# Forward FFT convolution: turning h and the tables on the matrix engine, groups in a written-out software pipeline, MLP weights loaded and turned meanwhile

## The chip, the cores and the metric

One core of one Trainium2 chip runs the whole program as one launch. The metric is the device time in microseconds (us). Five engines work from queues of their own: PE (matrix multiply, with its weight loads shown as PEld), DVE (vector), ACT (scalar, activation functions), POOL (general purpose) and SP (here only a queue that issues transfers). POOL issues transfers too. An engine runs its queue in order and waits on semaphores.

## What is computed

Sequence S=2048, width D=512, MLP width F=1376, bf16. Four layers with the same two sublayers, and the gradients of all inputs (11 outputs):

```python
def A(q, k, v, shift_k, ssm_k, ssm_D):     # q = layernorm(x)
    kv = causal_conv4(k, shift_k) * v
    y  = irfft(rfft(pad(kv)) * rfft(pad(ssm_k)))[:S]   # long convolution, 2S points
    return q * (y + kv * ssm_D)
def B(x): return gelu(x @ w1 + b1) @ w2 + b2
x = q
x = x + A(layernorm(x)); x = x + B(layernorm(x))
x = x + A(layernorm(x)); x = x + B(layernorm(x))
out, vjp = jax.vjp(f, all inputs); return out, *vjp(grad_out)
```

Since k, v and the filter h (`ssm_k`, given as D x S) do not depend on x, y is computed once and kept in SBUF as `y_res`.

## The kernel before

**Convolution forward** (`phase_conv_forward`). The transform of 4096 points is done by products with tables. `Fold` splits a signal's eight blocks into sums and differences (`fold_x`, `fold_s`, `fold_d`, `fold_t`); its `streams(k1)` gives the four operands for one residue class. The 16 tiles of frequencies lie in five `GROUPS` of 2, 2, 4, 4, 4 tiles. `fwd_group` multiplies a group's streams by a table into PSUM (`sp_ps`) and ACT evicts it (spectrum `Hg` of h, `KVg` of kv). `product` multiplies the two on DVE (`pr_t`, `pr_u`) into `Yg`; `inv_group` multiplies `Yg` by the inverse table `tabI` (`iv_ps`), evicted by ACT into the slots of `W`; `inv_blocks` and two more operations combine W into y on DVE.

The tables are sines, made by `sin_of` in pieces of 1024 columns: a multiply-add on POOL, a mask on DVE, a sine on ACT, through two buffers `tab_u`. `tabN` serves h, `tabF` serves kv. h must be read with time on partitions, and also reversed: it is turned by four transposing transfers, stored (`hT_d`), read back in flipped order (`hB_d`) and loaded. `tabI` (from `tabF_d`), `tabG` (for the backward, from `tabN_d`) and the turned k (`kT_d`) are made by four transposing transfers each, issued by SP, in `y_res` as scratch for the last two. In program order: tables, k slices (`kt_ps`: turn k; `ks_ps`: the four-tap filter as products with `wdiag`), kv, then all five H groups, stored to `Hspec_d`, then the five kv groups, each one whole: load H, spectrum, product, inverse. The order on each engine is set by the tile framework's scheduler.

**MLP forward and backward** (`phase_mlp`). `load_weights` loads w1, w2 and turns them by 15 transposing transfers on SP (L718, L720: `w2T_sb` in 11, `w1T_sb` in 4), then centres the rows of w1T on DVE (L724 to L726). `interleave` runs four token slices through the layers: layer norm (L757), turn n by transposing transfers (`nT_sl`), z, gelu, o, with n, h and gelu' stored to DRAM (`n_d`, `h_d`, `gp_d`). Then the output gradient is loaded into `G`, and the backward runs in the same way (`gT_sl`, `gh_ps`, `gz_sl`, L869).

**Convolution backward** (`conv_backward`) runs the same transforms for the gradients, with the weight gradients (`weight_grads`) put between its steps by hand; PE is pinned to program order there by `Ordered`. The gradient of the four-tap filter is 16 multiply-accumulates of 128 x 2048 on DVE (L612).

Of the kernel before, what the change touches and what calls it, by code (L numbers as in the profile page):

```python
# [11 lines left out]
ACT = mybir.ActivationFunctionType  # L12
# [59 lines left out]
def ssm_kernel(ctx, tc: tile.TileContext, aps: dict):  # L72
# [13 lines left out]
    dram.tabN = drampool.tile([P, 2, 2, 2048], BF16, name="tabN_d")  # L86
# [3 lines left out]
    dram.tabG = drampool.tile([P, 2, 16, 256], BF16, name="tabG_d")  # L90
    dram.kT = drampool.tile([P, ND, S], BF16, name="kT_d")
    dram.hT = drampool.tile([S + 1, D], BF16, name="hT_d")
    dram.ks = drampool.tile([P, NT, D], BF16, name="ks_d")
    for nm in ("vB", "qB", "goB", "hB", "o0B", "o1B", "o3B"):
        setattr(dram, nm, drampool.tile([4, 256, D], BF16, name=f"{nm}_d"))
# [4 lines left out]
    dram.gp = {li: drampool.tile([P, NFC, S], BF16, name=f"gp{li}_d") for li in (1, 3)}  # L100
    phase_conv_forward(nc, tc, dims, consts, dram, res, aps)
# [67 lines left out]
def sin_of(nc, consts, pool, out, krow, pv, shift, np_=P):  # L169
    n = krow.shape[-1]  # L170
    for c0 in range(0, n, 1024):
        w = min(1024, n - c0)
        u = pool.tile([P, 1024], I32, name="tab_u", tag="tab_u", bufs=2)[0:np_, 0:w]
        nc.gpsimd.tensor_scalar(out=u, in0=krow[:, c0:c0 + w], scalar1=pv, scalar2=float(shift), op0=ALU.mult,
                                op1=ALU.add)
        nc.vector.tensor_single_scalar(out=u, in_=u, scalar=8191, op=ALU.bitwise_and)
        nc.scalar.activation(out=out[:, c0:c0 + w], in_=u, func=ACT.Sin, scale=SIN_SCALE, bias=consts.pibias[0:np_, :])

# [25 lines left out]
class Fold:  # L204
# [14 lines left out]
    def streams(self, k1):  # L219
# [9 lines left out]
        if k1 == 1:  # L229
            nc.vector.tensor_scalar(out=D[:, :, 1], in0=D[:, :, 1], scalar1=C8, scalar2=None, op0=ALU.mult)  # L230
# [4 lines left out]
        tt(out=T[:, 0], in0=e0, in1=D[:, 0, 1], op=op)  # L235
        tt(out=T[:, 3], in0=o0, in1=D[:, 1, 1], op=op)
# [9 lines left out]
def fwd_group(nc, psum, tab, st, g, out, extra=None):  # L246
    k1, base, n = GROUPS[g]
    for mt in range(n):
# [19 lines left out]
        nc.scalar.activation(out=out[:, :, mt, :], in_=ps, func=ACT.Identity)  # L268


def product(nc, pool, A, B, Rb, g, out, conj):
# [4 lines left out]
    for h in range(0, n, 2):  # L276
# [3 lines left out]
        u = pool.tile([P, 2, 2, 512], BF16, name="pr_u", tag="pr_u", bufs=2)  # L280
# [46 lines left out]
def inv_blocks(nc, W, PN, MW, last=False):  # L327

    tt = nc.vector.tensor_tensor
    tt(out=PN, in0=W[:, :, 4:6], in1=W[:, :, 6:8], op=ALU.add)  # L330
    tt(out=MW, in0=W[:, :, 4:6], in1=W[:, :, 6:8], op=ALU.subtract)
    G, B0, B1 = W[:, :, 4:6], W[:, :, 6:8], W[:, :, 2:4]
    tt(out=G[:, :, 0], in0=W[:, :, 0], in1=W[:, :, 1], op=ALU.add)
    tt(out=G[:, :, 1], in0=W[:, :, 0], in1=W[:, :, 1], op=ALU.subtract)
    tt(out=B0, in0=G, in1=W[:, :, 2:4], op=ALU.add)
    tt(out=B1, in0=G, in1=W[:, :, 2:4], op=ALU.subtract)
    tt(out=G[:, :, 0], in0=PN[:, :, 1], in1=MW[:, :, 0], op=ALU.add)
    tt(out=G[:, :, 1], in0=PN[:, :, 1], in1=MW[:, :, 0], op=ALU.subtract)
    nc.vector.tensor_scalar(out=G, in0=G, scalar1=C8, scalar2=None, op0=ALU.mult)
    tt(out=W[:, :, 0], in0=B0[:, :, 0], in1=PN[:, :, 0], op=ALU.add)  # L340
    tt(out=W[:, :, 1], in0=B0[:, :, 1], in1=G[:, :, 0], op=ALU.add)
    tt(out=W[:, :, 2], in0=B1[:, :, 0], in1=MW[:, :, 1], op=ALU.add)
# [6 lines left out]
def phase_conv_forward(ctx, nc, tc, dims, consts, dram, res, aps):  # L349
# [4 lines left out]
    tt = nc.vector.tensor_tensor  # L354
    psum = ctx.enter_context(tc.tile_pool(name="cf_ps", bufs=1, space=bass.MemoryType.PSUM))
    rstack = ExitStack()
    tabs = rstack.enter_context(tc.tile_pool(name="cf_tab", bufs=1, side="right"))
    tabF = tabs.tile([P, 2, 2, 2048], BF16, name="tabF")
    kv = tabs.tile([P, NT, D], BF16, name="kv")
    hrot = rstack.enter_context(tc.tile_pool(name="cf_rot", bufs=1, side="right"))  # L360
    fold_stack = ExitStack()
    foldp = fold_stack.enter_context(tc.tile_pool(name="cf_fold", bufs=1, side="right"))

    gen = ExitStack()
    gp = gen.enter_context(tc.tile_pool(name="cf_gen", bufs=1))
# [7 lines left out]
    pv5 = iota_f32(nc, gp, [5, 1], [[0, 1]], -512, 1024, "pv5")  # L373
    nc.vector.memset(pv5[0:1, :], 0.0)
# [3 lines left out]
    hT = gp.tile([P, NT, D], BF16, name="hT")  # L378
    hB = gp.tile([P, 4, 2, D], BF16, name="hB")
    hsp = gp.tile([5, D], BF16, name="hsp")  # L380
    zrow = gp.tile([1, D], BF16, name="zrow")
    nc.vector.memset(zrow, 0.0)

    ks_stack = ExitStack()
    kp = ks_stack.enter_context(tc.tile_pool(name="cf_k", bufs=1))
    flip_rows(nc, dram.vB, v_ap, 511)
    kns = []
    for i in range(2):
        kns.append(kp.tile([P, 4, D], BF16, name="kn", tag="kn", bufs=2))
        nc.sync.dma_start(out=kns[i], in_=k_ap[512 * i:512 * i + 512, :].rearrange("(t p) d -> p t d", p=P))  # L390
    wsh = kp.tile([P, ND, 4], BF16, name="wsh")
    nc.sync.dma_start(out=wsh, in_=aps["A_shift_k"].rearrange("(c p) j -> p c j", p=P))
    for cc in range(ND):
        nc.sync.dma_start_transpose(out=hT[:, :, cc * P:(cc + 1) * P], in_=h_ap[cc * P:(cc + 1) * P, :])
    nc.sync.dma_start(out=dram.hT[S:S + 1, :], in_=zrow)
    nc.sync.dma_start(out=dram.hT[0:S, :].rearrange("(t p) d -> p t d", p=P), in_=hT)
    flip_rows(nc, dram.hB[1:4], dram.hT, 512)
    rs = dram.hT.ap[0][0]
    nc.sync.dma_start(out=dram.hB[0].rearrange("q (a c) -> a q c", a=2),
                      in_=bass.AP(tensor=dram.hT.tensor, offset=dram.hT.offset + S * rs,  # L400
                                  ap=[[256, 2], [-rs, 256], [1, 256]]))
    nc.sync.dma_start(out=hB, in_=dram.hB[:, :, :].rearrange("i (t p) d -> p i t d", p=P))
    nc.sync.dma_start(out=hsp[0:1, :], in_=aps["A_ssm_D"].rearrange("(o d) -> o d", o=1))
    nc.sync.dma_start(out=hsp[1:5, :], in_=dram.hT[0:S, :].rearrange("(i r) d -> i r d", r=512)[:, 256, :])
    nc.vector.memset(hB[0:1, :, 0, :], 0.0)

# [3 lines left out]
    for gi, (k1, base, n) in enumerate(GROUPS):  # L410
        for f in range(2):
            sin_of(nc, consts, gp, sp5[:, gi, f, :], krow[0:5, base * P:(base + 1) * P], pv5, 2048 * (1 - f), np_=5)
    nc.vector.memset(sp5[:, 0, 1, 0:1], 1.0)
    nc.vector.memset(altq, 0.0)
    nc.vector.tensor_copy(out=altq[:, 0:1], in_=consts.alt)
    nc.sync.dma_start(out=dram.tabN, in_=tabN)

    wshf = kp.tile([P, ND, 4], F32, name="wshf")
    nc.vector.tensor_copy(out=wshf, in_=wsh)
    wdiag = kp.tile([P, ND, 4, P], BF16, name="wdiag")  # L420
# [4 lines left out]
    nc.sync.dma_start(out=dram.wdiag, in_=wdiag)  # L425
    KA, KB, KW = 16, 272, 544
    kT = kp.tile([P, ND, 4, KW], BF16, name="kT")
    nc.vector.memset(kT[:, :, 0, 0:KA], 0.0)
    for i in range(4):
        if i >= 2:  # L430
            kns.append(kp.tile([P, 4, D], BF16, name="kn", tag="kn", bufs=2))
            nc.sync.dma_start(out=kns[i], in_=k_ap[512 * i:512 * i + 512, :].rearrange("(t p) d -> p t d", p=P))
# [7 lines left out]
        for j in range(1, 4):  # L440
            nc.vector.tensor_copy(out=kT[:, :, i, KB + 255 + j:KB + 256 + j], in_=kT[:, :, i, KA + 256 - j:KA + 257 - j])
            if i < 3:
                nc.vector.tensor_copy(out=kT[:, :, i + 1, KA - j:KA + 1 - j], in_=kT[:, :, i, KB + j - 1:KB + j])

    for qt in range(2):
        for f in range(2):
            sin_of(nc, consts, gp, tabF[:, f, qt, :], krow, pvh[:, qt:qt + 1], 2048 * (1 - f))
        nc.vector.tensor_copy(out=tabF[:, 1, qt, 0:1], in_=consts.alt)
    nc.sync.dma_start(out=dram.tabF, in_=tabF)

    for i in range(4):
        vt = kp.tile([P, 4, D], BF16, name="vt", tag="vt", bufs=2)
        tok_io(nc, vt, v_ap, dram.vB, i)
        ksb = kp.tile([P, 4, D], BF16, name="ksb", tag="ksb", bufs=2)
# [8 lines left out]
        nc.sync.dma_start(out=dram.ks[:, 4 * i:4 * i + 4, :], in_=ksb)  # L463
        tt(out=kv[:, 4 * i:4 * i + 4, :], in0=ksb, in1=vt, op=ALU.mult)

    hv = hT[:, :, :].rearrange("p (i h) d -> p i (h d)", i=4)[:, :, 0:2 * D]
    fh = Fold(nc, foldp, hv, hB[:, :, :, :].rearrange("p i h d -> p i (h d)"), True)
# [678 lines left out]
```

## Time and profile before

| | |
|---|---|
| median of the runs (three: 1137.49, 1141.8, 1150.26) | 1141.8 us |
| profiled execution | 1144.24 us, span 1142.4 us |
| PE, DVE, ACT, POOL busy, share of the span | 67%, 62%, 38%, 12% |
| mean granted clock of PE | 0.856 |
| bytes moved by transfers | 192.76 MB, mean 169 GB/s |
| convolution forward | 0 to 257.3 us |
| weights turned and centred | 257.3 to 290.8 us |
| MLP forward, backward | 290.8 to 553.0, to 761.6 us |
| convolution backward and weight gradients | 761.6 to 1142.4 us |

The span is the time from the first to the last instruction of the profiled execution; its own time holds some 2 us more. Engines overlap, so shares do not add up to one. A row of the timeline gives start, duration, engine, line and operation, and in brackets the engine's idle time before it and what ended it.

### The profile page before, as it was taken

The page shows a single profiled execution, that of the slowest core. Times are in us where ns is not written, and L with a number is a line of the kernel's source. Part 1 is how long each engine was busy: PE and PEld are TensorE (multiplying, and loading weights), DVE is VectorE, ACT ScalarE, POOL GpSimd, SP SyncE. Part 2 cuts the span into 40 slices and gives each one's busy share as a digit, 9 for nine tenths or more (in the row PEclk, how much of TensorE's full clock was granted, in tenths as well). Part 3 has the DMA queues.
Part 4 walks back from the last instruction along what each step waited for, and adds up shares of the span by engine and source line. Part 5 has one row for each costly group of instructions (what it writes and reads, how often), then busy time and mean ns, then how long its engine had stood idle before and what let it go on. Part 6 is the DMA issues. An engine that isn't in the chain of part 4 may idle for free.

```text
span 1142.4 us, 10702 instructions
## 1 busy us (share of the span) xinstructions
PE 767.5 (67%) x3745; PEld 345.7 (30%) x3745; DVE 706.6 (62%) x1353; ACT 439.4 (38%) x549; POOL 132.4 (12%) x221
## 2 busy tenths in 40 slices
PE   0419728710187888878489989863598966786994
PEld 0414203200032332323134333321143423542562
DVE  4334614581899999878268877890435662666752
ACT  5614314310198898899302222221052402310341
POOL 7300000000131110110000011120000103111000
PEclk9959858865588988999799999986698988897997
DMA  7465599317345564564867775428839699999930
GB/s 184 166 228 184 164 296 306 127 46 147 90 122 157 156 157 146 168 191 149 235 184 207 222 206 161 133 89 120 196 72 220 148 157 271 213 181 228 228 65 27
DMA packets 288078, 192.76 MB, mean 169 GB/s; under 512 B 186065, under 2 KB 276121, under 8 KB 287129
## 3 DMA queue, kind: packets, MB, share of 16 engines
q1 hardware_dynamic: 279673, 163.24, 58.5%
q0 software_dynamic: 7824, 28.85, 8.7%
q8 instruction: 29, 0.48, 0.2%
q14 instruction: 24, 0.20, 0.1%
q10 hardware_dynamic: 528, 0.00, 0.0%
HBM read 69.42 MB, written 87.24 MB: 137 GB/s over the span
## 4 chain that ended last, share of the span: by engine, by line
PE 21%; DVE 20%; DMA 15%; SPq 6%; ACT 6%; issue 5%; POOL 3%; DVEq 0%; ACTq 0%; POOLq 0%
PE dw_ps L55 7%; PE gh_ps L867 4%; DMA nb_sl<-n_d 3%; DMA ksb_b<-ks_d 2%; DVE ln_st L757 2%; SPq L956 2%; PE iv_ps L55 2%; PE gh_ps L55 2%; PE sp_ps L55 2%; DMA dw_tm<-h_d 2%; DVE g_o L818 2%; DVE gz_sl L869 2%; DMA o3B_d<-ksb_b 2%; DMA out_dram<-dw_oT 1%; DVE bb_junk L912 1%
## 5 line engine op out<-in xcount | busy, mean ns | idle before, releaser
L55 PE MATMUL dw_ps<-G,dw_tm 128*128 128x512 bf16 x704 | 170.7, 402 | 57.8 <-DMA dw_tm<-h_d 42.9
L848 PE MATMUL o_ps<-w_sb,h_sl 128*128 128x512 bf16 x352 | 96.0, 415 | 32.3 <-DVE h_sl L817 32.3
L55 PEld LDWEIGHTS <-dw_tm 128*128 128x128 bf16 x704 | 71.2, 103 | 148.1 <-DMA dw_tm<-h_d 41.0
L835 PE MATMUL z_ps<-nT_sl,w_sb 128*128 128x512 bf16 x352 | 84.7, 396 | 20.9 <-DMA nT_sl<-n_sl 20.5
L867 PE MATMUL gh_ps<-gT_sl,w2T_sb 128*128 128x512 bf16 x352 | 85.6, 396 | 19.4 <-DMA gT_sl<-G 16.5
L878 PE MATMUL gn_ps<-w1T_sb,gz_sl 128*128 128x512 bf16 x352 | 82.2, 379 | 0.1
L923 ACT ACTIVATE nb_sl<-nb_sl,ab_ab 128x512 bf16<-128x512 bf16 x32 | 23.4, 802 | 152.5 <-POOL ab_ab L921 80.8
L869 DVE SCALAR_TENSOR_TENSOR gz_sl<-gh_ps,gpb 128x512 bf16<-128x512 f32 x88 | 58.5, 688 | 26.2 <-PE gh_ps L867 25.6
L837 ACT ACTIVATE g_z<-z_ps,b1col 128x512 bf16<-128x512 f32 x88 | 54.5, 690 | 21.3 <-PE z_ps L835 21.3
L994 ACT ACTIVATE dw_o<-dw_ps 128x512 bf16<-128x512 f32 x22 | 13.1, 597 | 121.9 <-PE dw_ps L55 88.7
L848 PEld LDWEIGHTS <-h_sl 128*128 128x128 bf16 x352 | 34.0, 105 | 84.1 <-DVE h_sl L817 38.3
L845 PE MATMUL o_ps<-x_sl,ident 128*128 128x512 bf16 x32 | 13.0, 406 | 68.7 <-DVE x_sl L794 66.0
L835 PEld LDWEIGHTS <-w_sb 128*128 128x128 bf16 x352 | 35.0, 101 | 68.0 <-issue 21.0
L867 PEld LDWEIGHTS <-w2T_sb 128*128 128x128 bf16 x352 | 35.6, 102 | 64.4 <-issue 27.4
L771 ACT ACTIVATE n_sl<-x_sl,ln_nmr,rstd 128x512 bf16<-128x512 bf16 x32 | 24.7, 817 | 71.8 <-POOL ln_nmr L764 71.8
L612 DVE SCALAR_TENSOR_TENSOR Wb<-gksT,kTc 128x2048 bf16<-128x2048 bf16 x16 | 36.7, 2293 | 15.9 <-ACT gksT L589 13.7
L878 PEld LDWEIGHTS <-gz_sl 128*128 128x128 bf16 x352 | 34.4, 98 | 39.5 <-issue 0.4
L813 ACT ACTIVATE g_s<-g_t 128x2048 bf16<-128x2048 bf16 (+1 forms) x24 | 42.5, 1770 | 9.1 <-DVE g_t L812 9.0
L315 PE MATMUL iv_ps<-Yg,tabI 128*128 128x512 bf16 x56 | 20.4, 471 | 36.5 <-DVE Yg L287 32.2
L810 ACT ACTIVATE g_q<-g_z 128x2048 bf16<-128x2048 bf16 (+1 forms) x24 | 42.8, 1784 | 0.1
L814 ACT ACTIVATE g_o<-g_t 128x2048 bf16<-128x2048 bf16 (+1 forms) x24 | 42.4, 1765 | 0.0
L757 DVE BATCH_NORM_STATS2 ln_st<-x_sl 128x6 f32<-128x512 bf16 x64 | 41.9, 668 | 0.1
(279 smaller groups left out, 1392.5 us busy)
## 6 DMA issues: line engine op xcount, KB each, us to landing
n_d<-n_sl SPq DMA_DIRECT2D x16, 512.0 KB, 3.5
h_d<-h_sl SPq DMA_DIRECT2D x16, 512.0 KB, 2.9
gp_d<-g_p SPq DMA_DIRECT2D x16, 512.0 KB, 3.1
nb_sl<-n_d SPq DMA_DIRECT2D x16, 512.0 KB, 5.1
gpb<-gp_d SPq DMA_DIRECT2D x16, 512.0 KB, 5.9
gz_d<-gz_sl SPq DMA_DIRECT2D x16, 512.0 KB, 4.5
G<-n_d SPq DMA_DIRECT2D x2, 2048.0 KB, 17.7
Hspec_d<-Hg SPq DMA_DIRECT2D x3, 1024.0 KB, 4.3
```

What stands on the lines that cost most here:

```text
L55: return self.tc.keep_in_program_order(f(*args, **kwargs))
L612: nc.vector.scalar_tensor_tensor(out=junk, in0=gT[:, cc, 0:S], scalar=1.0, in1=kc[:, 16 - j:16 - j + S], op0=ALU.mult, op1=ALU.mult, accum ...
L757: nc.vector.bn_stats(out=st, in_=x[:, t, :])
L810: nc.scalar.activation(out=q, in_=zb, func=ACT.Square)
L813: nc.scalar.activation(out=sg, in_=t, func=ACT.Sigmoid)
L814: nc.scalar.activation(out=o, in_=t, func=ACT.Sigmoid, scale=-1.0)
L835: nc.tensor.matmul(ps, lhsT=w.w1[:, dc, c * P:(c + 1) * P], rhs=nT[:, dc, :], start=(dc == 0), stop=(dc == ND - 1))
L837: nc.scalar.activation(out=zb[:, c - c0, :], in_=ps, func=ACT.Identity, bias=w.b1col[:, c:c + 1])
L848: nc.tensor.matmul(ps, lhsT=h[:, c, t * P:(t + 1) * P], rhs=w.w2[:, c, :], start=False, stop=(c == NFC - 1))
L867: nc.tensor.matmul(ps, lhsT=w.w2T[:, dc, c * P:(c + 1) * P], rhs=gT[:, dc, :], start=(dc == 0), stop=(dc == ND - 1))
L869: nc.vector.scalar_tensor_tensor(out=gz[:, c, :], in0=ps, scalar=1.0, in1=gp[:, c - c0, :], op0=ALU.mult, op1=ALU.mult, accum_out=m.b1part ...
L878: nc.tensor.matmul(ps, lhsT=gz[:, c, t * P:(t + 1) * P], rhs=w.w1T[:, c, :], start=(c == 0), stop=(c == NFC - 1))
```

## The change

*h.* h is loaded as it is (`hN`); blocks of 128 x 128 are turned on PE by products with the identity and evicted by DVE (`hA`) and ACT (`hR`); `hR` is reversed by products with the reversing matrix and evicted by ACT (`hB`). No DRAM round trip.

*Tables.* `sin_of` does its second 1024 columns on DVE instead of POOL. `tabI` is turned on PE. `tabG` is computed in `conv_backward`. k's turned form is stored as it is in the front (`kT`, padded). Stores of ks, tabF, wdiag, kT and tabI go by POOL's queue.

*Order.* In `phase_conv_forward`, PE and DVE run in program order, which is now: h turned, Fold of h, k slices, H groups 0 and 1, ks slices, H group 2, tables tabF, H groups 3 and 4, weight loads, Fold of kv, tabI turned, and then the groups in a pipeline.

*Weights.* `start_weights` loads them in the front. `turn_weights` issues the 15 transposes as one more lane of the forward's `interleave` (from 60 units, 8 apart), SP in program order there. The centring stands behind the forward.

*Backward.* `inv_blocks` becomes `InvBlocks`, the same operations in pieces. The four-tap gradient runs in 32 halves; for its second half 32 extra turned blocks are written by PE and ACT (`gr_ps`).

```diff
 def sin_of(...)
-        nc.gpsimd.tensor_scalar(out=u, in0=krow[:, c0:c0 + w], scalar1=pv, ...)
+        eng = nc.gpsimd if c0 == 0 else nc.vector
+        eng.tensor_scalar(out=u, in0=krow[:, c0:c0 + w], scalar1=pv, ...)
...
+def turn_table(nc, psum, consts, tab, dest, f, qt):
+    for k0 in (0, 8):
+        ps = psum.tile([P, 8, P], BF16, name="tt_ps", tag="kt", bufs=2)
+        for k in range(8):
+            nc.tensor.transpose(out=ps[:, k, :], in_=tab[:, f, qt, (k0 + k) * P:(k0 + k + 1) * P], identity=consts.ident)
+        if f == 0:
+            nc.scalar.activation(out=dest(k0), in_=ps, func=ACT.Identity)
+        else:
+            nc.vector.tensor_copy(out=dest(k0), in_=ps)
...
 def phase_conv_forward(...)
+    nc = Ordered(nc, tc, ("tensor", "vector"))
...
-    for cc in range(ND):
-        nc.sync.dma_start_transpose(out=hT[:, :, cc * P:(cc + 1) * P], in_=h_ap[cc * P:(cc + 1) * P, :])
+    for cc in range(ND):
+        nc.sync.dma_start(out=hN[:, cc * S:(cc + 1) * S], in_=h_ap[cc * P:(cc + 1) * P, :])
...
+    for i in range(4):
+        k_slice(i)
+    h_group(0)
+    h_group(1)
+    for i in range(4):
+        ks_slice(i)
+    h_group(2)
...
+    h_group(3)
+    h_group(4)
+    res.w = start_weights(nc, wpool, dims, aps)
...
-    for g, (k1, base, n) in enumerate(GROUPS):
-        H = ...; nc.sync.dma_start(out=H, in_=dram.Hspec[...])
-        fwd_group(nc, psum, tabF, fk.streams(k1), g, KV)
-        product(nc, invp, KV, H, Rb, g, Y, False)
-        inv_group(nc, psum, tabI, Y, g, W)
+    sts = [fk.streams(GROUPS[0][0]), fk.streams(GROUPS[1][0])]
+    for g, (k1, base, n) in enumerate(GROUPS):
+        fwd_group(nc, psum, tabF, sts[g], g, KV)
+        if g:
+            inv_group(nc, psum, tabI, Ys[g - 1], g - 1, W)
+        product(nc, invp, KV, H, Rb, g, Ys[g], False)
+        if g + 2 < 5:
+            sts.append(fk.streams(GROUPS[g + 2][0]))
+    inv_group(nc, psum, tabI, Ys[4], 4, W)
...
 def conv_backward(...)
-        dma(out=tabG[:, :, :, 0:256], in_=dram.tabG)
+        for f in range(2):
+            for k0 in range(0, 16, 4):
+                for k in range(4):
+                    nc.gpsimd.tensor_scalar(out=u[:, k, :], in0=qrow, scalar1=kcol[:, k0 + k:k0 + k + 1], ...)
+                nc.vector.tensor_single_scalar(out=u, in_=u, scalar=8191, op=ALU.bitwise_and)
+                nc.scalar.activation(out=tabG[:, f, k0:k0 + 4, :], in_=u, func=ACT.Sin, ...)
...
+def turn_weights(order, w, wback, dims):
+    for c in range(NFC):
+        order.sync.dma_start_transpose(out=w.w2T[:, :, c * P:(c + 1) * P], in_=w.w2[:, c, :])
+        yield 8.0
+    for dc in range(ND):
+        order.sync.dma_start_transpose(out=w.w1T[:, :, dc * P:(dc + 1) * P], in_=w.w1[:, dc, :])
+        yield 8.0
...
 def phase_mlp(...)
-            interleave([(s * 12.0, fwd(s)) for s in range(NSL)])
+            interleave(lanes + [(60.0, turn_weights(Ordered(nc, tc, ("sync",)), m.w, wback, dims))])
+            centre_weights(nc, m.w, m.small, dims)
+        res.wstack.close()
```

DVE in the kv groups of the forward, before: the second half of group 2's product (`Hg_1092`), and the first two of the six operations of group 3's streams, with group 3's product behind them.

```order
L279 TENSOR_TENSOR pr_t<-KVg,Hg_1092 128x2048
L285 TENSOR_TENSOR pr_u<-KVg,Hg_1092 128x1024
L286 TENSOR_TENSOR pr_u<-KVg,Hg_1092 128x1024
L287 TENSOR_TENSOR Yg<-pr_t 128x1024
L288 TENSOR_TENSOR Yg<-pr_u 128x1024
L235 TENSOR_TENSOR fold_t<-fold_x,fold_d 128x1024
L236 TENSOR_TENSOR fold_t<-fold_x,fold_d 128x1024
```

And after, the end of group 1's product (`Hg_1143`), group 3's streams, the start of group 2's product (`Hg_1304`); the recorded line is that of the ordering helper.

```order
L55 TENSOR_TENSOR Yg<-pr_t 128x1024
L55 TENSOR_TENSOR Yg<-pr_u 128x1024
L55 TENSOR_SCALAR fold_s<-fold_d 128x2x1024
L55 TENSOR_SCALAR fold_s<-fold_s 128x1024 x2
L55 TENSOR_TENSOR fold_t<-fold_x,fold_s 128x1024 x2
L55 TENSOR_TENSOR fold_t<-fold_s,fold_x 128x1024 x2
L55 TENSOR_TENSOR pr_t<-KVg,Hg_1304 128x2048
```

Group 3's streams stand one group earlier, ahead of group 2's product. SP at the end of the MLP forward, before: the last stores of the forward, then the gradient's loads.

```order
L199 DMA out_dram<-x_sl 128x2x512
L841 DMA gp_d<-g_p 128x3x512
L199 DMA o0B_d<-x_sl 128x2x512
L201 DMA G_3479<-in_grad_out_dram 128x2x512
L201 DMA G_3479<-goB_d 128x2x512
```

After, at the same place:

```order
L209 DMA o0B_d<-x_sl 128x2x512
L55 DMA_TRANSPOSE w2T_sb<-w_sb 128x4x128
L55 DMA_TRANSPOSE w1T_sb<-w_sb 128x11x128 x4
L972 DMA gpb<-gp_d 128x4x512 x2
L211 DMA G_3677<-in_grad_out_dram 128x2x512
L211 DMA G_3677<-goB_d 128x2x512
```

The last five weight transposes and two loads of gelu' now stand ahead of the gradient's loads.

More of the change, by code (lines that the diff above doesn't have):

```diff
@@ L409, in phase_conv_forward @@
             sin_of(nc, consts, gp, tabN[:, f, qt, :], krow, pvn[:, qt:qt + 1], 2048 * (1 - f))
[L410 to L418, printed above, removed]
+    wshf = gp.tile([P, ND, 4], F32, name="wshf")
     nc.vector.tensor_copy(out=wshf, in_=wsh)
-    wdiag = kp.tile([P, ND, 4, P], BF16, name="wdiag")
+    wdiag = gp.tile([P, ND, 4, P], BF16, name="wdiag")
     for cc in range(ND):
@@ L424, in phase_conv_forward, with k_slice @@
                                     scalar2=None, op0=ALU.mult)
[L425 to L432, printed above, removed]
+    kT = gp.tile([P, ND, 4, KW], BF16, name="kT")
+    nc.vector.memset(kT[:, :, :, 0:KA], 0.0)
+    nc.vector.memset(kT[:, :, :, KB + 256:KW], 0.0)
+    def k_slice(i):
         for h in range(4):
@@ new lines, in phase_conv_forward @@
+    for cc in range(ND):
+        h_chunk(cc)
+    for m in range(2):
+        for i in range(4):
+            ps = psum.tile([P, 512], F32, name="hr_ps", tag="ks", bufs=2)
+            nc.tensor.matmul(ps, lhsT=consts.anti, rhs=hR[:, i, m * 512:(m + 1) * 512], start=True, stop=True)
+            nc.scalar.activation(out=hB[:, i, m * 512:(m + 1) * 512], in_=ps, func=ACT.Identity)
+    for gi, (k1, base, n) in enumerate(GROUPS):
+        for f in range(2):
+            sin_of(nc, consts, gp, sp5[:, gi, f, :], krow[0:5, base * P:(base + 1) * P], pv5, 2048 * (1 - f), np_=5)
@@ L476, in extra, with h_group @@
         return R, Z
[L478 to L482 removed]
+    def h_group(g):
+        k1, base, n = GROUPS[g]
+        st = fh.streams(k1)
+        for h0 in range(0, n, 2):
+            H = hrot.tile([P, 2, 2, 512], BF16, name="Hg", tag="Hg", bufs=2)
+            fwd_group(nc, psum, tabN, st, g, H, extra, h0, h0 + 2)
+            nc.sync.dma_start(out=dram.Hspec[:, :, base + h0:base + h0 + 2, :], in_=H)
@@ new lines, in phase_conv_forward @@
+    for i in range(4):
+        k_slice(i)
+    h_group(0)
+    h_group(1)
+    for i in range(4):
+        ks_slice(i)
+    h_group(2)
+    for qt in range(2):
+        for f in range(2):
+            sin_of(nc, consts, gp, tabF[:, f, qt, :], krow, pvh[:, qt:qt + 1], 2048 * (1 - f))
+        nc.vector.tensor_copy(out=tabF[:, 1, qt, 0:1], in_=consts.alt)
+    nc.gpsimd.dma_start(out=dram.tabF, in_=tabF)
+    nc.gpsimd.dma_start(out=dram.wdiag, in_=wdiag)
+    nc.gpsimd.dma_start(out=dram.kT, in_=kT)
@@ new lines, in phase_conv_forward @@
+    inv_group(nc, psum, tabI, Ys[4], 4, W)
+    yv = res.y[:, :, :].rearrange("p (i h) d -> p i h d", i=4)
+    px = foldp.tile([P, 2, 2, 2, 512], BF16, name="ibx", tag="fold_t", bufs=2)
+    ib = [InvBlocks(nc, W[m], tmp[m][:, 0], tmp[m][:, 1], px[:, m]) for m in range(2)]
+    for m in range(2):
+        ib[m].even()
+    for m in range(2):
+        ib[m].block0()
+        ib[m].out(0, yv[:, :, m], yv[:, :, 2 + m])
+    for m in range(2):
+        ib[m].others()
+        for i in range(1, 4):
+            ib[m].out(i, yv[:, :, m], yv[:, :, 2 + m])
@@ L1031, in phase_mlp @@
         nc.vector.memset(m.mhalf, -0.5)
[L1032 to L1034 removed]
+        with tc.tile_pool(name="m_g", bufs=2, reuse_waits="tile") as m.gpool:
+            m.w = res.w
             def fwd(s):
```

343 lines of the change are left out of this document (185 added, 158 removed).

## The prediction

> **What bounds the kernel now.** I read first the table of busy time by stretch, cut where the program changes stage (start and end us, length, busy us of PE, weight load, DVE, ACT and POOL with the instructions of each, granted clock, DMA share, GB/s).
>
> ```profile
> 0.00:74.80 74.80, 16.49 (x224) 15.27 (x225) 22.21 (x89) 36.81 (x51) 30.75 (x43) 0.89 0.58 170
> 74.80:92.10 17.30, 7.67 (x97) 7.66 (x97) 16.24 (x12) 4.07 (x7) 0.00 (x0) 0.58 0.71 262
> 92.10:132.50 40.40, 37.85 (x149) 11.48 (x147) 17.71 (x17) 15.85 (x16) 0.00 (x0) 1.00 0.47 172
> 132.50:235.20 102.70, 62.58 (x225) 23.40 (x224) 41.13 (x65) 34.05 (x39) 0.00 (x0) 0.75 0.81 237
> 235.20:257.30 22.10, 0.00 (x0) 0.00 (x0) 21.77 (x28) 0.00 (x0) 0.00 (x0) 0.60 0.00 0
> 257.30:290.80 33.50, 0.00 (x0) 0.00 (x0) 9.95 (x34) 0.00 (x0) 0.11 (x1) 0.50 0.68 149
> 290.80:553.00 262.20, 193.76 (x768) 75.09 (x768) 229.41 (x347) 214.74 (x229) 40.68 (x64) 0.88 0.51 150
> 553.00:761.60 208.60, 169.77 (x736) 71.15 (x737) 152.65 (x432) 41.15 (x57) 24.06 (x60) 0.93 0.68 185
> 761.60:1003.40 241.80, 174.71 (x954) 85.02 (x954) 118.09 (x173) 59.57 (x84) 27.43 (x40) 0.84 0.88 173
> ```
>
> One bound holds nowhere. The MLP forward (290.8 to 553) is a DVE and ACT stage, its backward (553 to 761.6) a PE stage, the convolution backward after it (with the weight gradients as filler) one of PE and transfers, and the change touches the arithmetic of the first two not at all. The 290.8 us ahead of them are serial: in 0 to 74.8 no engine is half busy, in 132.5 to 235.2 PE works 62.6 of 102.7 us, in 235.2 to 257.3 DVE alone, and in 257.3 to 290.8 nearly nothing. What fills that last hole stands in the chain that ended last (start, us, what):
>
> ```profile
> 257.29 1.26 SPq L718
> ...
> 270.39 1.27 SPq L718
> 271.71 1.45 SPq L720
> 273.20 1.69 SPq L720
> 274.94 1.65 SPq L720
> 276.63 4.07 DMA w1T_sb<-w_sb
> 280.89 1.29 DVE w1st L724 x2
> ```
>
> Fifteen weight transposes, one after the other on SP (eleven of 1.27 us, four of 1.6), a landing of 4.07, and from 280.9 ten us of centring on DVE, before the first layer norm starts at 290.8. Ahead of it, the waits of 132 to 235 us and the timeline say what idles PE and DVE there (DVE and PE waits: total, times, longest; timeline: start, us, engine and line):
>
> ```profile
> PE iv_ps L315 <- DVE Yg L287: 32.2, 8, 18.4
> DVE pr_t L279 <- ACT KVg L268: 30.6, 4, 13.1
> DVE pr_t L279 <- DMA Hg<-Hspec_d: 14.0, 1, 14.0
> 135.29 10.11 SPq L526 DMA_TRANSPOSE tabI<-tabF_d  x3
> 231.75 1.23 DVE L330 TENSOR_TENSOR ib<-W 128x2048 bf16<-128x2048 bf16 x1 [4.05 <-ACT W L324]
> ```
>
> PE waits for a group's product, DVE for the next group's spectrum: a ping-pong, with one 14 us stall because the load of the second H spectrum stands on SP behind the table transposes.
>
> **The change, part by part** (all against the profiled execution: span 1142.4, execution 1144.24, 2.4 above the 1141.8 median of the runs).
>
> *T1a, front up to the first H product.*
>
> ```profile
> 10.56 1.43 POOL L174 TENSOR_SCALAR tab_u<-krow,pvn 128x1024 int32<-128x1024 f32 x1 [0.29 <-ACT tabN L177]
> L439 ACT ACTIVATE kT<-kt_ps 128x512 bf16<-128x512 f32 x16 | 8.8, 594 | 16.0 <-PE kt_ps L436 16.0
> L177 ACT ACTIVATE sp<-tab_u,pibias 5x128 bf16<-5x128 int32 x10 | 4.0, 398 | 1.8 <-DVE tab_u L176 1.4
> 74.80 0.91 DVE L405 MEMSET hB<- 1x1024 uint32 x1 [3.53 <-DMA hB<-hB_d]
> 92.08 0.59 PE L267 MATMUL sp_ps<-fold_t,tabN 128*128 128x512 bf16 x2
> ```
>
> Before, the reversed h reaches DVE at 74.80, after transposes, a store, a flip and a load. Now it needs the plain load, then evictions. The sines of tabN keep their pace of 1.72 us each (1.43 + 0.29: POOL has to wait for ACT to read one of two buffers, and moving half its work to DVE leaves that loop as long), so the eight, begun near 7, end near 21; wdiag +3; four chunks with two PSUM evictions on DVE and two on ACT, at 0.59 each in turn, about 2.4: 33.5; eight reversals at 0.6: 38.5; the ten small sines on ACT and the kT evictions among them +6: 44.5. Fold and streams of h are the same DVE work as in 74.8 to 92.1 (16.2 us, kv products in it; without those about 10): first H product at **55**, 37 earlier.
>
> *T1b, from there to the first kv spectrum*, which before is at 132.5. Now everything that stood ahead comes behind: H products 37.9 us (the third stretch), ks products, eight sines of tabF, the table turning.
>
> ```profile
> 45.13 6.87 PE L460 MATMUL ks_ps<-wdiag,kT 128*128 128x128 bf16 x119
> L268 ACT ACTIVATE GY<-sp_ps 128x1024 bf16<-128x1024 f32 x16 | 16.2, 1023 | 29.2 <-PE sp_ps L55 29.2
> vt<-vB_d SPq DMA_DIRECT2D x4, 256.0 KB, 12.8
> ks_d<-ksb SPq DMA_DIRECT2D x4, 512.0 KB, 11.9
> ```
>
> 256 ks products at 6.87/119 are 14.8; the sines 8 x 1.72 = 13.8 (PE and DVE are pinned to program order, so later products queue behind); turning tabI is eight evictions of 1.02, half on ACT, half on DVE, in turn with PE through two buffers, 9; and waits: vt now stands on SP behind two Hspec stores and takes 12.8 to land, ksb has two buffers that each hold until an 11.9 us store lands. I take 10 for these. Sum 85: first kv spectrum at **140**, 7.5 later than before.
>
> *T1c, from there to the end of y*: 124.8 us before (132.5 to 257.3). Now group g+1's spectrum and group g-1's inverse lie beside group g's product. PE's 40.1 idle us (102.7 - 62.6) fall to some 12, since Yg has one buffer and its writer waits for the inverse before: -28. The busy 62.6 us were at a clock of 0.75; a kv group of four takes 7.07 when it runs undisturbed:
>
> ```profile
> 194.92 7.07 PE L267 MATMUL sp_ps<-fold_t,tabF 128*128 128x512 bf16 x32
> ```
>
> Three such and two halves are 25, the inverses a little more, 53 in all: -10. In the tail (231.75 to 257.3, 25.5 us) the `even` part, 7.6 us, now runs under the last inverse: -7. Together -45; y ends near 219. **T1 = 7.5 - 45 = -38.**
>
> *T2, the hole of 257.3 to 290.8.* Weights are loaded during the H groups and turned among the forward's transfers, so only the x load is left:
>
> ```profile
> x_sl<-qB_d SPq DMA_DIRECT2D x4, 256.0 KB, 4.7
> ```
>
> 33.5 - 5.1 = **T2 = -28.5.** The load was hidden by the centring; it is late next.
>
> *T3, forward to backward.* The last two w2T and the four w1T transposes now stand on SP ahead of the gradient's loads, which reuse the pool that the weights free and therefore wait for them.
>
> ```profile
> 550.84 0.44 SPq L199 DMA_DIRECT2D o0B_d<-x_sl  x1
> 553.04 0.37 SPq L201 DMA_DIRECT2D G<-in_grad_out_dram  x1
> 566.87 0.69 DVE L869 SCALAR_TENSOR_TENSOR gz_sl<-gh_ps,gpb 128x512 bf16<-128x512 f32 x1 [16.52 <-PE gh_ps L867]
> ```
>
> 2 x 1.27 + 6.4 + a landing of 4.07 = 13.0, of which the 2.2 us of idle SP between o0B and G take some: **T3 = +11.** The centring's ten us on DVE hide in the 16.5 us for which DVE waits there anyhow; without that cover +10.
>
> [...]
>
> *T4, nine w2T transposes among the forward's transfers.* SP is mostly idle there; the nearest rows are the same-shaped nT transposes and, at the far end, those of the busy weight-gradient stage (ns min/median/max):
>
> ```profile
> L800 SPq DMA_TRANSPOSE nT_sl<-n_sl x32: 1188/1220/2782, 306.2 to 510.2; - x32
> L956 SPq DMA_TRANSPOSE dw_tm<-h_d x22: 1968/2393/18658, 769.3 to 938.8; - x22
> ```
>
> From 0 (hidden behind DVE, 229 of 262 us busy) to 9 x 2.4 = 21. The shape decides for the first row: **T4 = +2.**
>
> *T5, convolution backward.* 32 more evictions on ACT (0.40 to 0.59 each by the two ACT rows of T1a: 13 to 19 us, with ACT a quarter busy in this stage), the shift-kernel gradient in 32 halves for 16 wholes (+2), and tabG computed where it was loaded:
>
> ```profile
> 1029.61 2.03 DVE L629 TENSOR_SCALAR tabG<-alt 128x1 bf16<-128x1 f32 x32 [11.80 <-DMA out_dram<-gwb]
> 1050.01 1.23 DVE L279 TENSOR_TENSOR pr_t<-GY,KVb 128x2048 bf16<-128x2048 bf16 x1 [8.79 <-DMA KVb<-KVspec_d]
> ```
>
> The 32 small DVE writes and a 2 MB load go (-2). In come 32 multiplies on POOL (272 of the 1024 columns of the 1.43 us row, 0.38 to 0.57 with a fixed part: 12 to 18 us), eight masks on DVE and eight sines on ACT (1.15 each). The table itself is wanted late, by the h gradient's inverse; but POOL also issues the KVb loads, which queue behind the multiplies, and DVE waits for such a load at 1050 already. So from -5 (the load's bandwidth freed) to +15 (all the multiplies on the path): **T5 = +5.**
>
> **Sum:** 1144.2 - 38 - 28.5 + 11 + 2 + 5 = 1095.7 beside the profiled execution, less 2.4: **1094 us**, 4.2% below the median.
>
> **The rivals.**
>
> *The pipeline is one in name (chance 0.12).* Yg has one buffer and all of PE and DVE stands in program order, so a late H load or KV eviction can stall both, and PE's waits may stay as now. For it: the 32.2 us of PE behind Yg. Against: the spectrum of the next group needs neither Y nor H. Then the -28 of T1c is lost: 1094 + 28 = 1122.
>
> *The front eats part (0.17).* Stores of ks, tabF, kT and wdiag go through POOL's queue, vt and Hspec through SP's, some 12 MB in 60 to 120 us; each of four vt and ks transfers may cost its whole 12 to 13 us instead of 10 in all: +15 to +25, about 1112. For it: the 12.8 and 11.9 us landings; against: they came about while 2 MB table moves shared the queues, which are gone.
>
> *Everything added is hidden (0.14).* T3, T4 and T5 vanish behind waits that are there anyway: 1094 - 18 = 1076.
>
> *Slower (0.04): the weight transposes stretch.* One mechanism: SP issues in order, so each w2T or w1T transpose that waits among the forward's n, h and gp transfers holds the nT transposes, which PE waits for, and then the gradient's loads. At the price of the forward's row nothing happens; in the weight-gradient stage the same kind went up to 18.7 us. The fifteen cost 14 us in my sum (T3, T4 and what is hidden). The gain of 48 is gone when each takes 48 / 15 = 3.2 us more on the path; at 8 us each, 1094 + 15 x 6.6 = 1193. Against: the DMA share of the forward is 0.51, that of the weight-gradient stage 0.88.
>
> **How the numbers follow.** My forecast has 0.53, and spans 1082 to 1108 (T1 by 10 either way from the 10 us of waits taken and the 12 us of PE idle, T4 and T5 by their ends). The range of eight in ten reaches from the hidden case to the lost pipeline: 1072 to 1122. About 1% either way is what a measurement of this kernel can tell from no change, 1130 to 1153. Faster by more holds in the forecast, the hidden case, most of the front and nearly all of the pipeline case: 0.90. Within 1%: 0.06, from pipeline and front together. Slower: 0.04.
>
> **What would show it.** T1a: the first product of fold_t and tabN near 55. T1b: the turning of tabF (tt_ps) until 140, with PE waiting in ks behind vt or ksb by some 10. T1c: no PE wait above 5 us on Yg, y's last write near 219, and the even sums beside the last inv_ps products. T2: the first layer norm within 6 us of that. T3: the gradient's first load about 13 us after the last gp store, and DVE's centring ended before the first gz. T4: w2T transposes of 1.2 to 2.8 us, the forward about 262 long. T5: the two backward convolution stretches together 381 +- 8. I am wrong if the first kv product comes after 155, if the forward grows by more than 10, or if the y end moves but the layer norm does not follow it.

## The result, and the profile after

The changed kernel takes **1090.15 us** (median of four runs, 1088.02 to 1094.82) against 1146.03 of the kernel before in the same comparison: ratio **0.9526**, 95% interval 0.9451 to 0.9600. 1094 was forecast. Ratios here and below leave out runs more than 1.5% above the fastest of the same kernel. The profiled execution is 1091.36 us, span 1089.6. Its table by stretch, cut at the events that answer to those of before (start and end, length, busy us of PE, weight load, DVE, ACT, POOL, granted clock, DMA share, GB/s):

```profile
0.00:51.40 51.40, 18.32 (x141) 13.08 (x142) 33.90 (x81) 32.36 (x52) 25.15 (x47) 0.87 0.32 113
51.40:142.50 91.10, 71.83 (x461) 34.63 (x465) 34.23 (x45) 38.19 (x44) 9.33 (x19) 0.79 0.58 206
142.50:219.80 77.30, 50.87 (x219) 21.99 (x223) 63.79 (x100) 32.70 (x38) 0.00 (x0) 0.89 0.32 122
219.80:222.60 2.80, 0.00 (x0) 0.00 (x0) 0.06 (x1) 0.00 (x0) 0.00 (x0) 0.50 0.47 158
222.60:480.70 258.10, 192.99 (x753) 74.86 (x768) 228.67 (x344) 212.28 (x225) 40.58 (x64) 0.87 0.54 161
480.70:507.60 26.90, 1.88 (x5) 0.74 (x6) 10.36 (x34) 5.81 (x9) 0.00 (x0) 0.59 1.08 251
507.60:699.00 191.40, 166.77 (x718) 70.38 (x731) 152.51 (x432) 38.07 (x52) 24.06 (x60) 0.96 0.63 179
```

The first H product comes at 51.4 (before 92.1), the first kv product at 142.5 (132.5), the end of y at 219.8 (257.3), the first layer norm at 222.6 (290.8), the last store of gelu' at 480.7 (550.4), the first gz at 507.6 (566.9), the bias products db_ps at 699.0 (761.6), the end at 1089.6 (1142.4). So the kernel gains 68.2 us up to the first layer norm and 1.4 in the MLP forward, pays 10.4 at the turn to the backward, is 3.4 shorter in the MLP backward, and pays 9.8 in the convolution backward: -52.8.

What replaced the hole and what the turn costs stands on SP's and DVE's timeline (start, us, line and operation, in brackets the idle time before it and its end):

```profile
219.94 0.40 SPq L211 DMA_DIRECT2D x_sl<-in_A_q_dram  x1
222.65 1.29 DVE L866 BATCH_NORM_STATS2 ln_st<-x_sl 128x6 f32<-128x512 bf16 x2 [2.69 <-DMA x_sl<-in_A_q_dram]
...
480.75 0.37 SPq L950 DMA_DIRECT2D gp_d<-g_p  x1
481.16 1.22 SPq L55 DMA_TRANSPOSE w2T_sb<-w_sb  x1
484.33 6.60 SPq L55 DMA_TRANSPOSE w1T_sb<-w_sb  x4
493.20 0.37 SPq L211 DMA_DIRECT2D G<-in_grad_out_dram  x1
507.62 0.69 DVE L978 SCALAR_TENSOR_TENSOR gz_sl<-gh_ps,gpb 128x512 bf16<-128x512 f32 x1 [4.01 <-PE gh_ps L976]
```

The x load is exposed for 2.7 us and nothing else. From the last gelu' store to the gradient's first load there are 12.4 us, 2.7 before, and DVE waits only 4.0 us for the first gz, since the centring lies in the rest.

### The profile page after: what moved, and what is told of

It is laid out like the page before. It is cut to its first block, busy times and chain, and to the rows that moved or that the text cites. A ratio compares the mean times of both kernels' runs of the same rounds, so it can differ in the third digit from the quotient of the medians.

```text
span 1089.6 us, 11131 instructions
## 1 busy us (share of the span) xinstructions
PE 785.0 (72%) x3856; PEld 359.2 (33%) x3917; DVE 728.8 (67%) x1373; ACT 468.8 (43%) x611; POOL 161.9 (15%) x281
## 5 line engine op out<-in xcount | busy, mean ns | idle before, releaser
L957 PE MATMUL o_ps<-w_sb,h_sl 128*128 128x512 bf16 x345 | 96.0, 420 | 34.2 <-DVE h_sl L926 33.5
L976 PE MATMUL gh_ps<-gT_sl,w2T_sb 128*128 128x512 bf16 x344 | 83.2, 390 | 29.6 <-DMA gT_sl<-G 26.6
L1103 ACT ACTIVATE dw_o<-dw_ps 128x512 bf16<-128x512 f32 x22 | 13.1, 596 | 130.7 <-PE dw_ps L55 91.7
L869 POOL TENSOR_SCALAR rstd<-ln_mv 128x4 f32<-128x4 f32 x16 | 11.5, 719 | 236.2 <-DVE ln_mv L867 153.0
L993 POOL TENSOR_SCALAR bb_diag<-ident,bb_cols 128x128 bf16<-128x128 bf16 x32 | 17.0, 530 | 182.7 <-DVE bb_junk L990 181.8
L55 PE MATMUL sp_ps<-fold_t,tabN 128*128 128x512 bf16 x85 | 30.2, 460 | 12.4 <-DVE fold_t L55 12.2
```

What stands on the lines that cost most here:

```text
L55: return self.tc.keep_in_program_order(f(*args, **kwargs))
L957: nc.tensor.matmul(ps, lhsT=h[:, c, t * P:(t + 1) * P], rhs=w.w2[:, c, :], start=False, stop=(c == NFC - 1))
L976: nc.tensor.matmul(ps, lhsT=w.w2T[:, dc, c * P:(c + 1) * P], rhs=gT[:, dc, :], start=(dc == 0), stop=(dc == ND - 1))
```

## The experiments

Stretches are read from one profiled execution of each kernel, medians and ratios from the timed runs. Profiled fronts of kernels with the same front code differ (the first kv product of the pinned kernels lies at 139.1 to 145.3, the end of y at 216.4 to 222.6), so a few us there prove nothing. Each kernel was timed beside the kernel before in a comparison of its own, and that kernel's median lay between 1141.0 and 1146.0 in them; so two medians from different comparisons can differ by some 5 us without a cause in the kernel.

**The weights part undone**, all else as after:

```diff
+            for _ in turn_weights(nc, m.w, wback, dims): pass
+            centre_weights(nc, m.w, m.small, dims)
...
-            interleave(lanes + [(60.0, turn_weights(...))])
-            centre_weights(nc, m.w, m.small, dims)
+            interleave(lanes)
```

> The changed kernel with the 15 transposes and the centring put back between the convolution forward and the MLP forward, loads of the weights still early. Theory (the hole was the transposes, a landing and the centring, 33.5 us against 2.8 us of x load now, and taking it away cost 10.4 us at the start of the backward): hole 28 to 34 us again, last gp store to first gz back to about 16.5 us, time 1090 + 29 - 10 = 1105 to 1111. Rival (the price at the backward is not the transposes): 1117 to 1121. Rival (the hole would shrink by itself since the weights are loaded early and SP is idle from 183 to 219 us): under 10 us, time 1085 to 1093.

Median 1115.66, ratio to before 0.9771 (0.9733 to 0.9809). Its timeline:

```profile
222.24 14.89 SPq L836 DMA_TRANSPOSE w2T_sb<-w_sb  x11
237.18 6.50 SPq L839 DMA_TRANSPOSE w1T_sb<-w_sb  x4
256.04 0.66 DVE L866 BATCH_NORM_STATS2 ln_st<-x_sl 128x6 f32<-128x512 bf16 x1
```

The hole is back at 34.0 us, and the turn to the backward is 17.0 us again (last gelu' store 514.2, first gz 531.1): both as the first theory had them. Its time is not: 1115.66 lies 4.7 above its range. Between the two profiled spans the difference is 24.4 us: 31.1 from the hole, less 9.9 at the turn, 2.3 in the front, which is within its spread, and 0.9 behind. The early loads did not shrink the hole, because the first transpose waited for the last write of y (SP's waits: total, times, longest):

```profile
SPq L836 <- DVE y_res L55: 33.7, 1, 33.7
```

**The weights part alone**, on the kernel before (transposes as a lane, centring behind the forward):

> The kernel before with the weights part alone: the 15 transposes as a lane of the MLP forward from 60 units on and 8 apart, the centring behind the forward; the convolution as before, weight loads where they were. Theory (this part by itself takes the hole of 33.5 us away and pays 10.4 us at the backward's start): 1141 - 28 + 10 = 1120 to 1126. Rival (the hole is then filled by the weight loads, which in this order land only near the end of the convolution, and by the bias loads): hole 8 to 15 us, time 1128 to 1135. Rival (the transposes in the forward hold the nT transposes when the forward starts earlier): above 1135.

Median 1120.33, ratio 0.9778 (0.9712 to 0.9844), about as the theory had it: this part by itself is worth 22 us by the medians and 25 by the ratio. Its profiled execution is the longest of the four (1131.30), so only the hole is read from it: y ends at 256.2, and the layer norm begins 3.1 us later:

```profile
259.23 1.29 DVE L768 BATCH_NORM_STATS2 ln_st<-x_sl 128x6 f32<-128x512 bf16 x2 [2.87 <-DMA x_sl<-in_A_q_dram]
```

**The kv groups in serial order again**, still pinned (`fk.streams`, `fwd_group`, `product`, `inv_group` in one loop):

> The changed kernel with the kv groups in serial order again (streams, spectrum, product, inverse, one group after the other), PE and DVE still pinned to program order, all else as after. Theory (the pipeline is what shortened the stretch from the first kv spectrum to the end of y from 124.8 to 77.3 us: PE works beside the product): 15 to 28 us are lost there, since in the trace before PE stood 32 us behind Yg, 14 of them for one H load that is gone either way; time 1105 to 1118. Rival (the gain came from the table transposes and the H load leaving SP, the pipeline only renames the order): the stretch stays within 8 us of 77, time 1090 to 1098.

Median 1114.80, ratio 0.9760 (0.9705 to 0.9816). From the first kv product to the end of y 99.2 us (139.8 to 239.0) against 77.3. The waits of that stretch, first in this kernel, then after (total, times, longest):

```profile
DVE pr_t L55 <- ACT KVg L278: 34.9, 5, 11.0
...
PE iv_ps L55 <- DVE Yg L55: 19.6, 8, 4.4
```

```profile
DVE Yg L55 <- PE iv_ps L55: 12.0, 3, 6.6
...
PE iv_ps L55 <- DVE Yg L55: 5.9, 3, 2.9
```

The ping-pong is back, without the 14 us stall of before. The pipeline is worth 22 of the 47 us that the stretch lost; in its place DVE now waits 12 us for Yg's one buffer, and PE 5.9 for Yg. Some ten of the 22 are not waits: PE's busy time for the same products is 61.2 us in the serial order, at a granted clock of 0.79, and 50.9 in the pipeline, at 0.89. The other 25 us of the 47 go with what else changed there (the 14 us stall behind the H load, the end of y partly under the last inverse); no run takes them apart.

**tabI turned by transfers again**, all else as after:

```diff
-            turn_table(nc, psum, consts, tabF, lambda k0: tabI[...], f, qt)
+            nc.sync.dma_start_transpose(out=tabI[:, f, :, qt * P:(qt + 1) * P], in_=dram.tabF[:, f, qt, :])
```

> The changed kernel with tabI turned by four transposing transfers from tabF's copy in DRAM, as before, instead of on PE. Theory (turning on PE stands on the path between the last H product and the first kv spectrum, 129.2 to 140.6 us, and only the first inverse needs the table; the transfers take 3.4 us each and land about 18 us after the last H store): first kv spectrum some 8 us earlier, the first inverse at about 150 as after, the end of y within 3 us of 219.8, time 1087 to 1093. Rival (turning on PE is worth what the table transposes cost before, where a spectrum's load stood 14 us behind them on SP): y ends 8 to 15 us later, time 1098 to 1105. Rival (transposing transfers are as quick as plain ones): y ends 5 us or more earlier, 1080 to 1085.

The first kv product came at 128.8, the first inverse at 142.5 (the first theory had it unchanged at 150), the end of y at 220.6, less than a us from after's. The 13.7 us won at the first kv product were lost again behind the first load of H and the transposed table (waits from 128.8 to 220.6):

```profile
DVE spec_rb L55 <- DMA Hg<-Hspec_d: 8.2, 1, 8.2
PEld L55 <- DMA tabI<-tabF_d: 6.0, 2, 5.0
PE iv_ps L55 <- DMA tabI<-tabF_d: 4.1, 1, 4.1
```

So for the end of y the first theory holds. The time, 1097.00, ratio 0.9634 (0.9563 to 0.9706), lies between its range and the first rival's: the convolution backward, which the edit does not touch, took 398.8 us from db_ps on against 390.6. There DVE waited 29.8 us for the ks loads (`ksb_b`), 19.0 in the changed kernel; why those loads came later stays open.

**The ks slices ahead of H groups 0 and 1** and **the tabF sines ahead of the ks slices**, two orders of the same front:

> The changed kernel with the four ks slices ahead of H groups 0 and 1 in program order, so that the vt loads stand ahead of the Hspec stores on SP and the ks products fill PE while DVE still folds h. Theory (in the front PE stands still some 17 us among the ks slices because vt and the two ksb buffers wait for transfers and stores, as the 10 us in my sum had it): first kv spectrum 5 to 10 us earlier than after (142.5), time 1080 to 1085. Rival (the front is held by ACT evictions and the tables, the ks waits only fill a gap): first kv spectrum within 3 us of after, time 1088 to 1092. Rival (the kv multiplies now queue on DVE behind the fold, ksb fills, and PE, in program order, holds the H products): later by 5 or more, 1095.

> The changed kernel with the sines of tabF ahead of the ks slices instead of behind H group 2. Theory (the front between the first H product and the first kv spectrum is held by the tabF sines: DVE waits 4.3 us for POOL, POOL 8.1 us for a sine that stands on ACT behind H evictions, and H group 3 waits behind both in program order): first kv spectrum 5 to 10 us earlier, 132 to 137, time 1081 to 1085. Rival (the ks slices wait for vt and the ksb stores, and this wait grows by what the tables gave): within 3 us of 142, time 1088 to 1092. Rival (the sines now stand ahead of the ksb evictions on ACT): later, 1092 to 1096.

The first gave 1089.36, ratio 0.9540 (0.9501 to 0.9578), first kv product 138.4, end of y 217.9: nothing gained that can be told from no change. The second gave 1099.25, ratio 0.9601 (0.9544 to 0.9659), first kv product 144.8, above every range that was forecast. PE now stood 8.6 us behind a ksb eviction. Of its 9 us only about 2 lie in the front; 6.7 lie in the convolution backward again (397.3 us; the wait for the ks loads is 26.4 there). Neither order took away the wait that it was meant to: PE's wait for ksb is 4.4 us in the changed kernel, 5.7 and 11.1 in these two. So they show no gain to be had by moving one block in the fixed order, and do not say by themselves what holds the front.

**PE and DVE left to the scheduler** in the convolution forward:

```diff
-    nc = Ordered(nc, tc, ("tensor", "vector"))
```

> The changed kernel with the convolution forward's PE and DVE left to the scheduler, the program's text unchanged. Theory (the written order, not the pinning, makes the pipeline, and the pinning costs in the front, where later products wait behind earlier ones that wait for transfers): y ends within 5 us of 219.8, time 1085 to 1095. Rival (the scheduler puts the products back in a serial order, as in the trace before): y ends 15 to 25 us later, time 1105 to 1115. Rival (the pinning holds the front): y ends 5 to 12 us earlier, 1078 to 1085.

Median **1067.04**, ratio 0.9381 (0.9322 to 0.9441): the third case, and more than it. The stretch from the first H product to the first kv product, here and then after, the H products alone (PE and ACT busy, clock, DMA share, GB/s), and the same of the kernel before:

```profile
44.00:107.20 63.20, 44.47 (x145) 15.22 (x16) 0.88 0.72 256
```

```profile
51.40:142.50 91.10, 49.00 (x141) 16.35 (x16) 0.79 0.58 206
```

```profile
92.00:132.50 40.50, 37.88 (x146) 15.25 (x15) 1.00 0.47 172
```

The scheduler puts ks products and part of the table turning between H products; PE is busy 58.4 of those 63.2 us, 71.8 of 91.1 when pinned. It turns part of the table after the first kv products, so the first inverse compares better: 130.7 against 148.8. y ends at 196.5, 23.3 us earlier, and the pipeline is kept without the pin: 89.3 us from first kv product to the end of y with most of the table turning in it. By the two profiled spans the pin costs 20.9 us, by the two medians 23, by the two ratios some 17.

**The gr_ps products left out:**

> The changed kernel without the gr_ps products and their 32 evictions in the convolution backward (the second halves of the four-tap gradient then read what W holds, so that output is left out). Theory (the time from the bias products of PE, db_ps, to the four-tap gradient's end grew by 7 us, and it is these 32 evictions on ACT and the 32 products that wait for the sp buffers): that time falls by 5 to 8 us, run 1082 to 1086. Rival (they hide beside PE's weight gradients; the halves on DVE and the order of the filler made the 7 us): within 2 us, 1088 to 1092.

1091.27, ratio 0.9548 (0.9486 to 0.9610); db_ps to the end of the four-tap gradient 263.3 us against 263.1, to the first h gradient product 318.7 against 317.0. The rival holds: the 32 evictions are hidden. The four-tap gradient still ends 7 us later than before (256.0), and no run here takes that apart.

**The multiplies of tabG on DVE:**

```diff
-                    nc.gpsimd.tensor_scalar(out=u[:, k, :], in0=qrow, scalar1=kcol[:, k0 + k:k0 + k + 1], ...)
+                    nc.vector.tensor_scalar(out=u[:, k, :], in0=qrow, scalar1=kcol[:, k0 + k:k0 + k + 1], ...)
```

> The changed kernel with the 32 multiplies of tabG in the convolution backward on DVE instead of POOL. Theory (they take 0.85 us each on POOL, the sines wait for them on ACT in order, and the eviction of a weight gradient waits behind a sine, which stops PE twice for 9 us): those two stops fall to 2 us, h gradient products start 4 to 10 us earlier, time 1081 to 1086. Rival (the products wait for the weight-gradient filler and the KVb loads, not for the table): 1088 to 1092. Rival (the multiplies delay the products of spectra on DVE): 1092 to 1096.

1085.85, ratio 0.9512 (0.9472 to 0.9553). The ratio alone cannot be told from the changed kernel's; the stretch can: db_ps to the end is 385.1 us, against 390.6 to 393.3 in seven kernels with the multiplies on POOL and more in the two named above. The changed kernel's trace shows why, on POOL, ACT and PE:

```profile
968.36 10.60 POOL L723 TENSOR_SCALAR tg_u<-qrow,kcol 128x272 int32<-128x272 f32 x12
...
997.95 1.20 ACT L726 ACTIVATE tabG<-tg_u,pibias 128x1088 bf16<-128x1088 int32 x1 [2.94 <-DVE tg_u L725]
999.05 0.58 ACT L1103 ACTIVATE dw_o<-dw_ps 128x512 bf16<-128x512 f32 x1
...
999.69 0.61 PE L55 MATMUL dw_pt<-ident,dw_o 128*128 128x128 bf16 x4 [8.36 <-ACT dw_o L1103]
```

One multiply takes 0.88 us on POOL. The eviction of a weight gradient (dw_o) stands behind a sine on ACT, and PE, done with it since 991, behind the eviction. This stop and one of 9.2 us before it fall to 1.0 and 5.6 us. The first h gradient product comes 301.2 us after db_ps instead of 317.0; of these 15.8 us the end sees 5.5, and PE now waits 7.3 us for DVE's products (`GY`).

**The weight transposes closer together**, first 4, then 2 units apart, the latter with tabG on DVE:

> The changed kernel with the weight transposes 4 instead of 8 units apart in the forward's lane, so that the last w1T transpose leaves SP about halfway through the MLP forward and the gradient's first load has nothing of the weights ahead of it. Theory (the six transposes and their landing on SP between the forward's last store and the gradient's loads are the whole price of the move, 10.4 us in the trace after): last gp store to first gz back to about 16.5 us, or 26 at most if the centring (10 us on DVE) loses its cover; the forward as long as after (258 us); time near 1080. Rival (the price only moves: SP issues in order, so transposes packed closer hold the nT transposes that PE waits for): the forward grows by 6 to 20 us, time 1087 to 1100. Rival (the gradient's loads wait for the freed memory anyway): 1090, unchanged.

> The changed kernel with the weight transposes 2 units apart (the last w1T transpose then leaves SP well ahead of the forward's last stores, not among them as with 4) and the multiplies of tabG on DVE. Theory (the two prices paid by the change, 10.4 us at the backward's start and 5.6 us for the table on POOL, are separate and both avoidable): last gp store to first gz 16.5 us, forward no longer than 260 us, db_ps to the end 385 us; time 1075 to 1080, below both kernels. Rival (packed transposes hold the nT transposes): the forward 3 to 12 us longer, time 1081 to 1090. Rival (with the backward starting earlier its own loads collide): first gz earlier but db_ps not, 1084 to 1088.

At 4 the last w1T transpose still left SP at 479.0, behind the last gelu' store; the turn fell from 26.9 to 18.5 us in the profile (1083.22), but the median of six, 1089.82, ratio 0.9542 (0.9499 to 0.9584), shows no gain. Two of its six runs took 1082 and 1083, the other four 1089 to 1095, and only one of the two is profiled, so where the others lost it is not known. At 2:

```profile
479.73 0.37 SPq L950 DMA_DIRECT2D gp_d<-g_p  x1
480.57 0.37 SPq L209 DMA_DIRECT2D o0B_d<-x_sl  x1
482.42 0.37 SPq L211 DMA_DIRECT2D G<-in_grad_out_dram  x1
```

No weight transpose stands between the stores and the gradient; the turn is 16.7 us, the forward 259.6, db_ps to the end 385.1. Median 1076.60, ratio 0.9462 (0.9412 to 0.9511): 13.5 us below the changed kernel, the sum of the two prices within 2.5. Spacing 2 was not run without the tabG edit; beside that edit alone it is 9.2 us.

**All three edits:**

> The changed kernel with the three edits together: PE and DVE of the convolution forward left to the scheduler, the weight transposes 2 units apart, the multiplies of tabG on DVE. Theory (three separate prices, in the front, at the backward's start and in the convolution backward, so the gains add: 23 us from the order, 13.5 from the other two): first layer norm near 200, last gp store to first gz 17 us, db_ps to the end 385 us; time 1050 to 1058. Rival (they share a wait, so that the earlier forward runs into the transposes or the filler): 1060 to 1067.

Median **1056.93** (1054.98 to 1064.56), ratio 0.9252 (0.9203 to 0.9301): the best version, 33 us below the changed kernel; the turn is 16.6 us here, the first layer norm at 199.0. The prices are nearly separate: 33.2 of the 36.7 us to which they add up by the medians. The rest fits the convolution backward, which took 388.6 us and not the 385 forecast.

## Why the prediction was right

By its own steps: **T1** -38, measured -37.5. **T2** -28.5, measured -30.7: the x load cost 2.8 us, not 5.1, because the norm starts on the first of its pieces. **T3** +11, measured +10.4 at the place named, with the centring hidden as said; the MLP backward was 3.4 us shorter, which the sum did not have. **T4** +2, measured -1.4. **T5** +5, measured +9.8, past the +-8 that I gave for the stretch. That the total lies within 4 us is in part luck: T5 is 4.8 short, and T4 and the MLP backward give back 6.8 that the sum did not have and that no run explains. (Its last line, 1095.7 less 2.4, is 1093.3, not 1094.) The undone and isolated parts (weights 22 to 25 us, pipeline 22 to 25) bear out the mechanisms and not only the sum.

Two steps were wrong inside. *T1b* came out near its total (91.1 us for 85) with other terms: I had 37.9 us of H products, the figure of an unbroken stretch at full clock, and 10 us of waits for vt and ksb. The H products took 49.0, in a stretch with a granted clock of 0.79. PE stood idle 19.3 us, of which 4.4 behind ksb, none behind vt, some 9.6 behind DVE's streams (`fold_t`) and 4.6 behind the table's evictions. Two other orders gained nothing; without the fixed order y ends 23 us earlier. My rival "the front eats part" named transfers; what the runs show is the price of the pin. That the front loses 10 us against before although h is there 41 us earlier I had at 7.5. *T5*: I named the 32 multiplies and the wrong queue. I took 0.38 to 0.57 us each and KVb's issue behind them; they take 0.88, and the path is ACT's order, sine ahead of eviction. With the multiplies on DVE the stretch is still 4.3 us longer than before, and no run shows why. The gr evictions, which I had counted as a possible price, cost nothing.

## What to carry to other kernels

A serial hole between stages (loads, transposes, a fix-up) can be worth nearly its whole length (here 30.7 of 33.5 us) when its work fits a queue that is idle elsewhere, but see that the last piece leaves that queue before the next stage's loads: here the spacing decided 10 us of the turn. Write the pipeline as program order, and test the pin separately: the same text without it was 17 to 23 us faster. In the front PE then stood idle 4.8 us instead of 19.3, and its granted clock was 0.88 instead of 0.79. A cheap-looking table on an idle engine is priced by whoever evicts behind it (here tabG on POOL, 5.5 us at the end).

## What the runs showed of the hardware that I had not expected

PE's granted clock changed between half and full again and again in the front (stretch, PE busy, granted clock, DMA share, GB/s, in the changed kernel):

```profile
52.30:58.30 6.00, 5.98 (x13) 0.50 0.59 252
59.00:70.60 11.60, 11.57 (x169) 1.00 0.78 243
75.80:78.50 2.70, 2.70 (x29) 0.50 1.08 373
79.50:82.00 2.50, 2.50 (x47) 1.00 1.07 344
84.40:86.50 2.10, 2.10 (x8) 0.88 0.82 261
87.00:96.00 9.00, 9.00 (x20) 0.50 0.39 141
96.50:99.10 2.60, 2.60 (x11) 1.00 0.21 77
104.00:113.00 9.00, 8.19 (x17) 0.50 0.67 264
114.00:130.00 16.00, 15.95 (x73) 1.00 0.38 141
```

Four products of 512 columns took 1.89 us at the half clock and 1.04 at the full one. By these two times the 25.7 us of H products that ran at half (6.9, 10.2 and 8.5 up to 58.7, 96.2 and 113.3) would have been some 12 us shorter at the full clock, an estimate; beyond the 37.9 of before the H products take 11.1. The changes lie on a grid: worked out from the mean clock of short stretches across them, they come at 58.7, 75.8, 79.2, 86.0, 96.2, 103.1 and 113.3, each a whole multiple of 3.4 us after the one before, to 0.1 us. So the third H group, 2.3 us after the last ks product, began at full speed and fell to half only at 86.0, with PE at work. From 75.8 the clock was back at full after one step, at 79.2; from 86.0 and from 103.1 it took three. Why PE ran at half for three steps from 86.0, busy throughout, stays open.

Three small POOL copies took 0.48 us before DVE's fold of h, and 4.46 and 5.61 us beside it (POOL's timeline after):

```profile
36.98 0.48 POOL L454 COPY kT<-kT 128x4 bf16<-128x4 bf16 x3
41.38 4.46 POOL L454 COPY kT<-kT 128x4 bf16<-128x4 bf16 x3
45.77 5.61 POOL L456 COPY kT<-kT 128x4 bf16<-128x4 bf16 x3
```

DVE added tensors from 41.16 to 52.45; the next three copies, at 52.70, took 0.44 us again. The rows show that the two fall together; no run here took the cause apart.
